# A planned transformer kernel: unread matmuls by share of the array, a finer table for VectorE's banks, a reserve behind a bank's last operation

## The chip, the core and the metric

The kernel runs on one core of a Trainium2 chip. The metric is the device time of one execution in microseconds; the table below gives three runs of the kernel before. TensorE (PE) multiplies matrices into PSUM, ScalarE (ACT) does the exponentials, VectorE (DVE) copies, adds and normalizes, GpSimd (POOL) takes a small share, and SyncE (SP) issues DMA transfers. Each engine works through its own queue in order.

## The reference

Two layers over a sequence of 2048 tokens of 448 numbers, each of an attention part with 16 heads of 28 and a dense part with a hidden width of 1792, both behind a layer norm and added to their input. The same weights serve both layers.

```python
def _A_ref(x, wqkv, wo):
    ...
    q, k, v = qkv[0], qkv[1], qkv[2]
    scores = jnp.einsum("bhqd,bhkd->bhqk", q, k) * Dh ** -0.5
    p = _softmax(scores, axis=-1)
    o = jnp.einsum("bhqk,bhkd->bhqd", p, v)
    return (lambda x, *d: x.transpose(*d))(o, 0, 2, 1, 3).reshape(B, S, D) @ wo

def _B_ref(x, w1, b1, w2, b2):
    h = jnp.einsum("bsd,df->bsf", x, w1) + b1
    r = jnp.where(h > zero, h, zero)
    h = r * r
    return jnp.einsum("bsf,fd->bsd", h, w2) + b2

x = A_x
x = x + _A_ref(_layernorm(x, axis=-1), A_wqkv, A_wo)
x = x + _B_ref(_layernorm(x, axis=-1), B_w1, B_b1, B_w2, B_b2)
x = x + _A_ref(_layernorm(x, axis=-1), A_wqkv, A_wo)
x = x + _B_ref(_layernorm(x, axis=-1), B_w1, B_b1, B_w2, B_b2)
```

## The kernel before

**Units, groups and banks.** The queries are cut into blocks of 256 (the last two of layer 1 of 128). A *unit* is 512 columns of scores: one head, one block of queries and two tiles of 128 keys (four tiles in the 128-query blocks). There are 2048 units in all, 1024 for each layer. A unit's scores fill one bank of PSUM. `s_stream` (L859) issues the score matmuls of a *group* of three units at a time (L924). A head has 28 numbers, padded to 32, so a score matmul uses 32 of the array's 128 rows, and those of different heads lie in different strips of rows. `e_stream` (L940) lets ScalarE compute the exponential of the group's banks in one instruction (L954). `p_stream` (L1044) multiplies the exponentials with the values, four heads side by side in strips of 32 columns (L1095), and one more column of ones gives the sums of the softmax.

**Banks that go to VectorE.** ScalarE need not take all three banks: `apart` (L815) decides, as a group is issued, whether a third unit is handed to VectorE. Then ScalarE's instruction has two banks. `a_unit` (L995) and `a_rest` (L1012) compute that bank's exponential with bit arithmetic: a shift and a maximum on VectorE (L1002), a product on GpSimd (L1019), a square (L1025) and a final sum on VectorE (L1032). Among the conditions of `apart` are a free set of scratch buffers, a busy share of VectorE of at most `BUSY` over 11 us, no bank among the last `STOP` units, and the table: `PACE[i * len(PACE) // len(units)]` (L840), in us, is the most that VectorE's backlog may hold when unit i is issued. With 64 entries, one holds for 32 units.

**The order of work.** The program is laid out by a planner (`Planner`, L140) while it is built. Every piece of work is an `Op` with an engine, a planned duration, what it depends on and which buffer it takes and releases. Streams of ops stand side by side with priorities (scores 0, exponentials 1, attention-value 2, then normalization, projections and dense parts, `sums` 9.1, `heat` 9.5); `run` (L193) takes again and again the op that can start first by the planner's own clocks. `earliest` (L163) computes when an op's inputs are there: the end of each, its `lat`, and a latency of its engine. Two ops with `port=True` on VectorE and GpSimd are not planned at the same time. The order so found is the order of each engine's queue; on the chip the engines then wait for each other by semaphores. So a changed planned duration changes no instruction, only the order.

**Dense work.** `layernorm` (L520), `qkv` (L681), `chain` (L1234) and `mm_tile` (L634, matmuls at L655) do the projections and the dense part of a block of tokens while the attention of other blocks goes on. VectorE copies their results out of PSUM: keys at L678, queries at L674, values at L706, relu at L1289, the square at L1296, the residual sum at L1231. `sums` (L375) adds up the columns of w1 for the tail, with matmuls against a single column of ones (L387), once the queries of layer 1 are there.

**Unread matmuls.** The planner adds matmuls that nobody reads. First, `s_stream` can issue the score matmuls of a group up to `MORE` = 3 more times into the same banks, where TensorE would be idle anyway and the exponentials of the group before still run (L911 to L916). Second, `heat` (L1501) issues one or two matmuls into a spare bank behind a group (L1516). Both look at `load` (L154), TensorE's planned busy share over the last microseconds: repetitions below 0.9 over 3.4 us (0.8 for the last 100 units), `heat` below 0.76 over 2.8 us.

**The tail.** After the last group of scores `finish` (L1329) and `ends_last` (L1436) carry the last block through its projection, norm and dense part.

Of the kernel before, what the change touches and what calls it, by code (L numbers as in the profile page):

```python
# [26 lines left out]
GY = 0.65  # L27
# [17 lines left out]
ENDU = 100  # L45
HOTE = 0.8
# [9 lines left out]
WINDOW = 2.8  # L56
# [19 lines left out]
PACE = (3.6, 2.2, 2.2, 1.8, 1.8, 1.8, 1.8, 3.0, 0.3, 0.9, 2.2, 2.2, 2.2, 1.4, 1.4, 1.4, 1.4, 1.4, 1.4, 2.2, 2.2, 2.2, 2.2, 1.4, 3.0, 3.0, 2.2, 2.2, 2.2, 1.8, 4.5, 4.5, 2.6, 2.6, 3.0, 3.0, 3.0, 3.6, 3.0, 1.4, 3.0, 4.5, 4.5, 4.5, 1.4, 1.4, 0.9, 1.4, 0.3, 1.4, 1.4, 1.4, 2.2, 2.2, 1.8, 1.8, 1.8, 1.8, 2.6, 2.6, 1.8, 1.8, 0.3, 6.0)  # L76
# [4 lines left out]
HOT = 0.9  # L81
MORE = 3
HEAT = 0.76
HWIN = 3.4
# [39 lines left out]
class Op:  # L124
    __slots__ = ("eng", "dur", "fn", "deps", "acq", "rel", "mode", "sets", "start", "end", "res", "turn", "ready", "lat", "need", "got", "more", "room", "port")

    def __init__(self, eng, dur, fn, deps=(), acq=None, rel=None, mode="full", sets=(), lat=0.0, need=1, port=False):
        self.eng = eng if isinstance(eng, tuple) else (eng,)
        self.dur, self.fn, self.deps, self.mode, self.lat = dur, fn, deps, mode, lat
        self.rel = rel if isinstance(rel, list) else ([] if rel is None else [rel])  # L130
        self.acq = acq if isinstance(acq, tuple) or callable(acq) else (() if acq is None else (acq,))
        self.sets = sets if isinstance(sets, list) else ([sets] if sets else [])
        self.start = self.end = self.res = self.turn = None
        self.need, self.got, self.more, self.port = need, [], 0.0, port
# [5 lines left out]
class Planner:  # L140
# [3 lines left out]
    def __init__(self):  # L144
        self.clock = {"PE": 0.0, "ACT": 0.0, "DVE": 0.0, "POOL": 0.0, "DMA": 0.0, "-": 0.0}
        self.mode = None
        self.tok = {}
        self.streams = []
        self.past = {"PE": [], "DVE": []}
        self.ports = {"POOL": [], "DVE": []}  # L150
        self.turns = lambda: False
        self.slack = lambda: SLACK
# [5 lines left out]

    def spawn(self, prio, gen):
        self.streams.append([prio, gen, next(gen, None)])  # L160
        self.streams.sort(key=lambda s: s[0](0.0) if callable(s[0]) else s[0])

    def earliest(self, o):  # L163
        t = 0.0
        for d in o.deps:
            if not isinstance(d, Op):
                d = self.tok.get(d)
            if d is None or d.end is None:
                return None, None
            same = d.eng[0] == o.eng[0] and len(o.eng) == 1  # L170
            t = max(t, d.end + d.lat + ((0.03 if same else 0.10) if d.eng[0] == "DVE" else
                                (0.0 if same and d.eng[0] != "DMA" else LAT[d.eng[0]])))
# [20 lines left out]
    def run(self):  # L193
        while self.streams:
# [46 lines left out]
def kernel(  # L241
# [278 lines left out]
    def layernorm(t0, nt, deps_of, early=False, mv=None, place=None, x_in=None, parts=False):  # L520
# [9 lines left out]
        for a, b in [(0, 1), (1, 2)] if single else [(0, nt)]:  # L530
# [9 lines left out]
            pl.spawn(EV, iter([rs]))  # L540
        box = {}
# [68 lines left out]
        for p0 in range(0, nt, wide):  # L610
# [4 lines left out]
            for j in js:  # L615
                xn = xns[2 * (own.turn % 2) + j % 2]

                def norm(e, j=j, xn=xn):
                    nc.vector.tensor_scalar(out=xn[:, 0:D], in0=x_sb[:, t0 + j, :],  # L619
                                            scalar1=mv[0][:, j, 0:1], scalar2=ln[j],  # L620
                                            op0=ALU.subtract, op1=ALU.mult)
                nm = Op("DVE", 0.39, norm, deps=[rss[j], *([] if x_in is None else [x_in])], sets=[("n", t0, j)] if early else (), port=True)
                yield nm
                xs.append((xn, nm))
# [234 lines left out]
    def s_stream():  # L859
        while at[0] < len(units):  # L860
# [5 lines left out]
            def fn(e, gi=gi, us=us, js=js):  # L866
# [44 lines left out]
                short = (HOT if len(units) - at[0] > ENDU else HOTE) - pl.load(HWIN)  # L911
# [4 lines left out]
                o.more = 0.22 * again  # L916
                for i in list(range(4)) * (again + 1):
# [94 lines left out]
    def a_rest(gi, c, box, unit):  # L1012
# [7 lines left out]
        y = Op("POOL", GY, part, deps=[c, ("p", gi)] if own else [c], acq=None if own else lambda: pd_free(unit), port=True)  # L1020
# [13 lines left out]
        o = Op("DVE", 0.683, close, deps=[h], rel=c, sets=("x", gi), port=True)  # L1034
# [9 lines left out]
    def p_stream():  # L1044


        for pi, (l, qb, g, kbs, first, last) in enumerate(passes):
# [19 lines left out]
            while todo:  # L1067
# [16 lines left out]
                def fn(e, now=now, begin=begin, close=close, box=box, pi=pi, l=l, g=g, r=r, n=n):  # L1084
# [4 lines left out]
                    for kb in now:  # L1089
# [15 lines left out]
                       rel=[gbuf[gi]["p" if w == "e" or gbuf[gi]["in"] else w] for w, gi in by], mode="col")  # L1105
                box.setdefault("o", o)
# [79 lines left out]
    def norm_pair(l, qb, g, pair):  # L1186
# [34 lines left out]
        def mul(e):  # L1221
            nc.vector.tensor_tensor(out=oTn_of[l, qb][0][:, g:g + 2, 0:n], in0=both,  # L1222
                                    in1=box["r"][:, :, 0:n], op=ALU.mult)
        m = Op("DVE", 0.13 + 2 * n / 930, mul, deps=[r, oTn_of[l, qb][1]], rel=pair["own"], port=True)
# [9 lines left out]
    def chain(l, qb):  # L1234
# [43 lines left out]
        for f0 in range(0, NFC, pack):  # L1278
# [11 lines left out]
            def square(e, b=b, w=w, f0=f0):  # L1290
                r = b["r"][:, 0:w].rearrange("p (f q) -> p f q", q=n)
                b["h"] = h = hidden(f0 // pack)
                if e == "ACT":
# [4 lines left out]
            def then(o, b=b, square=square):  # L1298
                aside = not s_left and (l, qb) == (1, len(blocks[1]) - 2)
                b["s"] = Op("ACT" if aside else "DVE", 0.5 if aside else 0.42, square, deps=[o], rel=o, port=True)  # L1300
# [200 lines left out]
    def heat():  # L1501


        for gi in itertools.count(HFROM):
# [63 lines left out]
```

## Time and profile before

| what | us |
|---|---|
| three runs: median (lowest, highest) | 845.75 (845.54, 848.41) |
| the profiled execution | 845.42 |
| its span, first to last instruction | 843.6 |
| ScalarE busy in the span | 821.3 |
| TensorE busy | 806.6 |
| VectorE busy | 783.8 |
| GpSimd busy | 225.3 |
| HBM traffic | 19 GB/s, mean over the span |

The mean clock granted to TensorE is 0.994 of the full one. The profile has views that the text uses: the busy shares of the engines; groups of instructions by line and shape (busy time, mean duration of one, idle time of the engine before them and what ended it); the span cut into stretches (busy time and count for each engine, granted clock, DMA); the waits in total; and the instructions in order of time. The names are those of the program: `sc` scores, `pt` exponentials, `oT` attention output, `mt` a dense result, `v_w` the scratch of a bank on VectorE. PEld is the loading of weights, which goes beside matmuls.

### The profile page before, as it was taken

What the parts mean: (1) busy time and instruction counts of PE and PEld (TensorE: products, weight loads), DVE (VectorE), ACT (ScalarE), POOL (GpSimd) and SP (SyncE); (2) the same over time, 40 slices, a digit from 0 to 9 for tenths busy, and PEclk for the clock granted to TensorE, in tenths of its full rate; (3) what the DMA queues carried; (4) which work ended last, traced back from release to release, by engine and by line L of the source; (5) the groups of instructions that cost most, each with busy time, mean ns of one, the idle gap of its engine ahead of it and who ended that gap; (6) DMA issues with size and microseconds to landing.
All of it is one profiled execution on the core that took longest, in us unless ns stands there. A gap on an engine that the chain in (4) does not pass through costs nothing.

```text
span 843.6 us, 28341 instructions
## 1 busy us (share of the span) xinstructions
PE 806.6 (96%) x12255; PEld 428.6 (51%) x12255; DVE 783.8 (93%) x1610; ACT 821.3 (97%) x700; POOL 225.3 (27%) x354
## 2 busy tenths in 40 slices
PE   8999999999999999999999999989999999999997
PEld 4455545554545455455445444534554545545565
DVE  7999989999989999999999999989989999999955
ACT  8998999999999999999999999989999999999994
POOL 3222322223222233222332333332222222232300
PEclk9999999999999999999999999989999999999999
DMA  9200000000000000000000000011000000000000
GB/s 251 68 3 2 25 20 15 16 15 15 15 3 16 15 15 16 7 11 15 2 2 3 2 2 3 11 30 32 18 23 21 20 26 15 14 25 16 17 11 18
DMA packets 32365, 17.98 MB, mean 21 GB/s; under 512 B 17833, under 2 KB 31787, under 8 KB 32240
## 3 DMA queue, kind: packets, MB, share of 16 engines
q1 hardware_dynamic: 32240, 16.18, 6.9%
q8 instruction: 95, 1.56, 0.8%
q14 instruction: 30, 0.25, 0.1%
HBM read 13.88 MB, written 2.07 MB: 19 GB/s over the span
## 4 chain that ended last, share of the span: by engine, by line
PE 44%; DVE 27%; ACT 22%; issue 5%; DMA 1%; POOL 0%; SPq 0%; ACTq 0%; DVEq 0%
ACT pt L954 22%; PE mt L655 18%; PE sc L924 15%; PE oT L1095 8%; DVE v_w L1002 3%; DVE pt L1032 2%; DVE r L1289 2%; DVE V_sb L1032 2%; DVE K_sb L1002 2%; DVE pt L1025 2%; DVE V_sb L1025 1%; PE mt L1516 1%; DVE xn L619 1%; DVE oTn L1222 1%; DVE Q_sb L674 1%
## 5 line engine op out<-in xcount | busy, mean ns | idle before, releaser
L954 ACT ACTIVATE pt<-sc 128x1536 bf16<-128x1536 f32 (+1 forms) x683 | 810.0, 1377 | 9.1 <-PE sc L924 8.0
L924 PE MATMUL sc<-Q_sb,K_sb 32*128 32x256 bf16 (+1 forms) x5258 | 308.6, 267 | 22.3 <-ACT pt L954 17.1
L924 PEld LDWEIGHTS <-K_sb 32*128 32x128 bf16 x5258 | 131.1, 92 | 202.5 <-issue 157.5
L1095 PE MATMUL oT<-pt,V_sb 128*32 128x256 bf16 (+1 forms) x4008 | 154.2, 270 | 1.2 <-DVE pt L1032 0.7
L1002 DVE TENSOR_SCALAR v_w<-sc 128x512 f32<-128x512 f32 x187 | 127.4, 683 | 10.7 <-PE sc L924 9.9
L655 PE MATMUL mt<-xnT,w 128*128 128x256 bf16 (+1 forms) x888 | 118.6, 271 | 0.9 <-DVE xnT L571 0.4
L1095 PEld LDWEIGHTS <-V_sb 128*32 128x32 bf16 x4352 | 91.4, 96 | 50.9 <-issue 47.7
L655 PEld LDWEIGHTS <-w 128*128 128x128 bf16 x896 | 74.9, 98 | 35.6 <-issue 27.3
L1019 POOL TENSOR_SCALAR V_sb<-v_w 128x512 bf16<-128x512 uint16 x74 | 54.2, 733 | 131.1 <-DVE v_w L1002 130.3
L1289 DVE TENSOR_SCALAR r<-mt 128x512 bf16<-128x512 f32 x108 | 73.9, 684 | 6.3 <-PE mt L655 5.9
L1019 POOL TENSOR_SCALAR pt<-v_w 128x512 bf16<-128x512 uint16 x69 | 46.2, 670 | 114.0 <-DVE v_w L1002 91.4
L655 PE MATMUL mt<-w,V_sb 128*128 128x448 bf16 (+1 forms) x288 | 70.5, 349 | 0.0
L1002 DVE TENSOR_SCALAR K_sb<-sc 128x512 f32<-128x512 f32 x73 | 49.8, 683 | 4.6 <-PE sc L924 4.5
L1032 DVE SCALAR_TENSOR_TENSOR V_sb<-v_w,V_sb 128x512 int16<-128x512 f32 x74 | 51.5, 698 | 0.1
L1032 DVE SCALAR_TENSOR_TENSOR pt<-v_w,pt 128x512 int16<-128x512 f32 x69 | 47.7, 694 | 0.1
L1231 DVE TENSOR_TENSOR x_sb<-x_sb,mt 128x448 bf16<-128x448 bf16 x62 | 37.9, 612 | 8.7 <-PE mt L655 8.4
L1025 DVE TENSOR_TENSOR pt<-pt 128x512 bf16<-128x512 bf16 x99 | 45.1, 468 | 0.7 <-POOL pt L1019 0.7
L1025 DVE TENSOR_TENSOR V_sb<-V_sb 128x512 bf16<-128x512 bf16 x89 | 41.4, 474 | 2.5 <-POOL V_sb L1019 2.5
L1019 POOL TENSOR_SCALAR pt<-K_sb 128x512 bf16<-128x512 uint16 x30 | 21.6, 719 | 71.9 <-DVE K_sb L1002 51.5
L509 DVE BATCH_NORM_STATS2 st<-x_sb 128x6 f32<-128x448 bf16 x63 | 38.7, 616 | 1.2 <-DMA x_sb<-in_A_x_dram 0.7
L1516 PE MATMUL mt<-xn,ident 128*128 128x448 bf16 x105 | 36.5, 364 | 0.9 <-DVE oT_sb L1123 0.3
L655 PEld LDWEIGHTS <-V_sb 128*128 128x128 bf16 x302 | 24.3, 98 | 25.2 <-issue 12.1
(143 smaller groups left out, 882.1 us busy)
## 6 DMA issues: line engine op xcount, KB each, us to landing
rec<-scr SPq DMA_DIRECT2D x54, 128.0 KB
x_sb<-in_A_x_dram SPq DMA_DIRECT2D x8, 224.0 KB
out_dram<-x_sb SPq DMA_DIRECT2D x15, 112.0 KB
w<-in_B_w_dram SPq DMA_DIRECT2D x1, 1568.0 KB
w<-in_B_w_dram SPq DMA_DIRECT2D x1, 1344.0 KB
dn<-oT_sb SPq DMA_DIRECT2D x54, 4.0 KB
V_sb<-in_A_wqkv_dram SPq DMA_DIRECT2D x4, 168.0 KB
scr<-dn SPq DMA_DIRECT2D x27, 8.0 KB
```

Source lines behind the costliest of these rows:

```text
L509: nc.vector.bn_stats(out=box["st"][:, :], in_=x_sb[:, t0 + j, :] if src is None else src())
L655: nc.tensor.matmul(box["t"][:, c0:c0 + n], lhsT=lhsT() if callable(lhsT) else lhsT, rhs=rhs, start=a, stop=b)
L924: nc.tensor.matmul(dst[k][:, i * nt * P:(i + 1) * nt * P], lhsT=K_sb[l][rows, g, (kb + i) * P:(kb + i + 1) * P], rhs=Q_sb[rows, g, t0 * P: ...
L954: t = nc.scalar.activation(out=pt[:, 0:n], in_=gbuf[gi]["sc"][:, 0:n], func=AF.Exp, scale=float(np.log(2.0)) * 2.0 ** -FRAC)
L1002: t = nc.vector.tensor_scalar(out=box["w"], in0=two(src), scalar1=EXP_SHIFT, scalar2=EXP_LOW, op0=ALU.add, op1=ALU.max)
L1019: nc.gpsimd.tensor_scalar(out=two(pd), in0=low, scalar1=-EXP_MID * 65536, scalar2=EXP_BEND, op0=ALU.add, op1=ALU.mult)
L1025: nc.vector.tensor_tensor(out=pd, in0=pd, in1=pd, op=ALU.mult)
L1032: nc.vector.scalar_tensor_tensor(out=two(pd.bitcast(DT.int16)), in0=box["w"], scalar=EXP_BITS, in1=two(pd), op0=ALU.add, op1=ALU.add)
L1095: nc.tensor.matmul(box["t"][DHP * hh:DHP * hh + DHP, 0:n], lhsT=V_sb[l][:, kb + i, 4 * g + hh, :], rhs=p[:, c0:c0 + n], start=begin and kb ...
L1231: nc.vector.tensor_tensor(out=x_sb[:, tb, lo:hi], in0=x_sb[:, tb, lo:hi], in1=t[:, 0:hi - lo], op=ALU.add)
L1289: nc.vector.tensor_scalar(out=r[:, 0:w], in0=t[:, 0:w], scalar1=0.0, scalar2=None, op0=ALU.max)
L1516: nc.tensor.matmul(t[:, 0:D], lhsT=ident[:, :], rhs=xns[0][:, 0:D], start=True, stop=True)
```

## The change

Three things change in the planner's decisions.

- Unread matmuls: `load` is replaced by `warm`, the share of the array used over the last `TICK` = 1.8 us of the plan. Each op on TensorE adds a weight `w`: 0.0533 us for each unit of scores and each pass, 0.2133 for each step of attention-value, and 0.9 (`SHARE`) of the planned duration for every other op. Both kinds of unread matmuls are added below 0.55 (`WARM`, `WARM2`).
- The table `PACE` has 128 entries in place of 64, with other values; one now holds for 16 units.
- Planned times in `a_rest`: the product on GpSimd takes 0.617 in place of 0.65 with 0.05 behind it (`YL`), and the last sum on VectorE has 0.25 behind it (`XL`), which counts for what reads it and for the buffers that it releases.

`earliest` keeps the time of an op's inputs once it is known. Options to put the norm, the pair product and some squares on GpSimd come in and are off (`NORMG`, `GM_ON`, `GS_ON` = 0).

```diff
-GY = 0.65
+GY = 0.617
+XL = 0.25
+TICK = 1.8
+WARM = 0.55
+WARM2 = 0.55
+SHARE = 0.9
+YL = 0.05
...
-PACE = (3.6, 2.2, 2.2, 1.8, 1.8, 1.8, 1.8, 3.0, 0.3, 0.9, 2.2, 2.2, 2.2, 1.4, 1.4, 1.4, 1.4, 1.4, 1.4, 2.2, 2.2, 2.2, 2.2, 1.4, 3.0, 3.0, 2.2, 2.2, 2.2, 1.8, 4.5, 4.5, 2.6, 2.6, 3.0, 3.0, 3.0, 3.6, 3.0, 1.4, 3.0, 4.5, 4.5, 4.5, 1.4, 1.4, 0.9, 1.4, 0.3, 1.4, 1.4, 1.4, 2.2, 2.2, 1.8, 1.8, 1.8, 1.8, 2.6, 2.6, 1.8, 1.8, 0.3, 6.0)
+PACE = (2.2, 2.2, 2.2, 2.2, 1.8, 2.2, 2.2, 1.4, 3.0, 1.4, 1.4, 1.4, 2.2, 3.2, 3.6, 2.2, 2.2, 2.2, 2.2, 2.2, 0.6, 3.4, 2.6, 1.8, 1.0, 1.8, 2.6, 2.6, 2.2, 3.8, 3.0, 2.2, 2.2, 3.6, 2.2, 0.6, 3.0, 1.8, 1.8, 1.8, 1.8, 2.6, 2.2, 2.2, 1.4, 3.4, 2.6, 1.0, 2.2, 3.4, 3.6, 3.6, 1.4, 2.2, 3.0, 2.6, 3.8, 3.4, 1.8, 1.0, 2.6, 2.6, 2.2, 2.2, 3.8, 3.0, 1.8, 1.0, 3.8, 3.0, 1.8, 2.2, 2.2, 1.4, 3.2, 4.4, 2.6, 3.6, 3.6, 1.4, 1.8, 3.6, 3.0, 3.0, 3.0, 3.0, 2.2, 2.2, 2.2, 2.2, 3.0, 3.0, 1.8, 2.2, 2.6, 2.6, 1.4, 1.4, 4.0, 3.6, 3.6, 1.8, 1.8, 2.2, 2.2, 3.6, 1.4, 1.4, 2.2, 4.0, 1.8, 1.4, 2.2, 1.8, 2.6, 2.6, 2.2, 2.2, 2.6, 2.2, 2.8, 3.2, 1.4, 1.8, 1.8, 2.2, 2.2, 2.2)
...
+    def warm(self):
+
+        now = self.clock["PE"]
+        return sum(w * (min(e, now) - max(s, now - TICK)) / (e - s) for s, e, w in self.used if e > now - TICK and s < now) / TICK
...
+            if e == "PE" and o.end > s:
+                self.used = [u for u in self.used if u[1] > s - 2 * TICK] + [(s, o.end, SHARE * o.dur if o.w is None else o.w)]
...
-                short = (HOT if len(units) - at[0] > ENDU else HOTE) - pl.load(HWIN)
+                short = WARM2 - pl.warm()
...
+                o.w = 0.0533 * len(us) * (again + 1)
...
-        y = Op("POOL", GY, part, deps=[c, ("p", gi)] if own else [c], acq=None if own else lambda: pd_free(unit), port=True)
+        y = Op("POOL", GY, part, deps=[c, ("p", gi)] if own else [c], acq=None if own else lambda: pd_free(unit), port=True, lat=YL)
...
-        o = Op("DVE", 0.683, close, deps=[h], rel=c, sets=("x", gi), port=True)
+        o = Op("DVE", 0.683, close, deps=[h], rel=c, sets=("x", gi), port=True, lat=XL)
...
+                o.w = 0.2133 * len(now)
...
-            short = HEAT - pl.load(WINDOW)
+            short = WARM - pl.warm()
...
-            k = 1 if short < 0.14 else 2
+            k = 1 if short < 0.055 else 2
```

More of the change, by code (lines that the diff above doesn't have):

```diff
@@ L149, in __init__ @@
         self.past = {"PE": [], "DVE": []}
+        self.used = []
         self.ports = {"POOL": [], "DVE": []}
@@ L163, in earliest @@
     def earliest(self, o):
[L164 to L172, printed above, removed]
+        t = o.base
+        if t is None:
+            t = 0.0
+            for d in o.deps:
+                if not isinstance(d, Op):
+                    d = self.tok.get(d)
+                if d is None or d.end is None:
+                    return None, None
+                same = d.eng[0] == o.eng[0] and len(o.eng) == 1
+                t = max(t, d.end + d.lat + ((0.03 if same else 0.10) if d.eng[0] == "DVE" else
+                                    (0.0 if same and d.eng[0] != "DMA" else LAT[d.eng[0]])))
+            o.base = t
         acq = o.acq() if callable(o.acq) else o.acq
@@ L540, in layernorm, with turned @@
             pl.spawn(EV, iter([rs]))
+            if not parts and NORMG and not early:
+                def turned(e, a=a, b=b):
+                    ln["m"] = mv[0][:, 2:4, 0]
+                    nc.vector.tensor_scalar(out=ln["m"][:, a:b], in0=mv[0][:, a:b, 0], scalar1=-1.0, scalar2=None, op0=ALU.mult)
+                ng = Op("DVE", 0.165, turned, deps=[mv[1][b - 1]])
+                yield ng
         box = {}
```

37 lines of the change are left out of this document (24 added, 13 removed).

## The prediction

> **What bounds the kernel now.** I read the busy shares and the waits first, then the groups by form, then the span cut into stretches. All durations are those of the profiled execution, 845.42 us, of which the span is 843.6 and 1.8 lies around it; the median of the runs is 845.75, so a gain found in the span is taken off 845.75 unchanged.
>
> ```profile
> PE 806.6 (96%) x12255; PEld 428.6 (51%) x12255; DVE 783.8 (93%) x1610; ACT 821.3 (97%) x700; POOL 225.3 (27%) x354
> ...
> L954 ACT ACTIVATE pt<-sc 128x1536 bf16<-128x1536 f32 (+1 forms) x683 | 810.0, 1377 | 9.1 <-PE sc L924 8.0
> ```
> ```profile
> L954 ACT ACTIVATE pt<-sc 128x1536 bf16<-128x1536 f32 x422 | 607.8, 1541 | 4.7 <-PE sc L924 4.0 <-PE oT L1095 0.3
> L924 PE MATMUL sc<-Q_sb,K_sb 32*128 32x256 bf16 x4746 | 291.5, 273 | 20.0 <-ACT pt L954 15.0 <-DVE K_sb L1002 1.1 <-DVE oTn L1222 0.5
> L954 ACT ACTIVATE pt<-sc 128x1024 bf16<-128x1024 f32 x261 | 278.7, 1113 | 4.4 <-PE sc L924 4.0 <-ACT pt L954 0.3
> ...
> L1516 PE MATMUL mt<-xn,ident 128*128 128x448 bf16 x105 | 36.5, 364 | 0.9 <-DVE oT_sb L1123 0.3 <-DVE V_sb L706 0.2 <-DVE more L1121 0.2
> ```
>
> ScalarE sets the time. It runs 683 groups of exponentials, 422 over three banks and 261 over two; the third bank of each of those 261 went to VectorE. A group always takes three units, so the count of groups is fixed (2048 units), and the only thing that shortens ScalarE's own work is the number of two-bank groups: each one more is worth 1541 - 1113 = 428 ns.
>
> ```profile
> 10.70:63.90 53.20, 51.88 (x736) 27.31 (x733) 51.04 (x117) 53.09 (x43) 12.49 (x25) 1.00 0.30 86
> 63.90:117.30 53.40, 50.91 (x759) 28.21 (x760) 51.95 (x102) 50.15 (x44) 14.75 (x20) 1.00 0.05 13
> 117.30:168.50 51.20, 48.76 (x752) 26.44 (x748) 46.31 (x95) 50.74 (x44) 12.08 (x20) 1.00 0.07 18
> 168.50:220.20 51.70, 50.57 (x760) 26.99 (x752) 49.51 (x100) 51.45 (x44) 13.24 (x22) 1.00 0.05 13
> 220.20:271.30 51.10, 49.71 (x753) 26.46 (x747) 45.90 (x92) 51.10 (x44) 13.73 (x22) 1.00 0.05 13
> 271.30:320.80 49.50, 47.76 (x707) 24.83 (x703) 48.13 (x98) 49.50 (x43) 14.32 (x25) 1.00 0.05 13
> ...
> 371.90:423.30 51.40, 48.76 (x748) 25.79 (x741) 50.26 (x105) 50.37 (x44) 15.81 (x22) 1.00 0.03 7
> 423.30:472.50 49.20, 47.40 (x711) 24.22 (x710) 47.82 (x95) 48.88 (x43) 14.53 (x23) 1.00 0.01 2
> ...
> 523.00:573.80 50.80, 47.11 (x690) 22.41 (x690) 47.13 (x97) 48.61 (x44) 18.97 (x27) 0.90 0.08 19
> 573.80:624.70 50.90, 48.52 (x741) 24.54 (x742) 48.17 (x99) 50.88 (x44) 11.21 (x17) 1.00 0.10 27
> 624.70:675.80 51.10, 49.66 (x732) 27.01 (x724) 47.00 (x93) 51.10 (x44) 11.96 (x18) 1.00 0.07 19
> ...
> 726.40:775.50 49.10, 47.83 (x708) 25.07 (x701) 47.89 (x98) 49.10 (x43) 12.35 (x19) 1.00 0.06 18
> ...
> 829.20:843.60 14.40, 10.72 (x133) 7.82 (x130) 7.56 (x26) 3.08 (x7) 0.56 (x1) 1.00 0.06 18
> ```
>
> These stretches are sixteenths of the units (some 43 groups each); after the length come the busy times of PE, PEld, DVE, ACT and POOL, then the clock. From 10.7 to 829.2 us the exponentials take 810.0 (both forms with their overlaps removed, the page's row of L954); so only about 818.5 - 810.0 = 8.5 us of ScalarE are idle there, and they sit in few places: 3.25 in the stretch from 63.9, 1.03 in that from 371.9, 2.19 in that from 523.0. The 10.7 us ahead and the 14.4 behind are the start and the tail. TensorE's 96% is no bound: part of it is matmuls that nobody reads.
>
> ```profile
> ACT pt L954 <- PE sc L924: 8.0, 12, 3.1
> ```
> ```profile
> 67.48 9.76 ACT L954 ACTIVATE pt<-sc 128x1536 bf16<-128x1536 f32 x8
> 80.34 1.94 ACT L954 ACTIVATE pt<-sc 128x1024 bf16<-128x1024 f32 x2 [3.10 <-PE sc L924]
> ```
> ```profile
> 79.19 0.69 DVE L678 CAST K_sb<-mt 128x512 bf16<-128x512 f32 x1 [0.19 <-PE mt L655]
> ```
>
> All waits of ScalarE's exponentials for scores come to 8.0 us in 12 places, and one of them is 3.10: the scores issued at 79.84 need keys that VectorE copies at 79.19 to 79.88.
>
> **Change, part 1: unread matmuls.** Their number is in the rows above. The 256-column score matmuls needed are 2 for each of 1920 units (the other 128 units lie in blocks of one row tile and use the 128-column form), 3840; 4746 were issued, so 906 are repetitions, about 151 passes of six. To them come 105 of L1516. A repeated pass costs
>
> ```profile
> 69.18 0.40 PE L924 MATMUL sc<-Q_sb,K_sb 32*128 32x256 bf16 x6 [0.25 <-ACT pt L954]
> ...
> 70.24 0.83 PE L924 MATMUL sc<-Q_sb,K_sb 32*128 32x256 bf16 x18
> ```
>
> (0.83 - 0.40) / 2 = 0.22 us, so 33 us, and the 105 about 36.5 us of busy time, of which some goes beside other work. The new rule asks not how long PE was busy but how much of the array's rows and columns it used over 1.8 us, and adds below 0.55. Counted so (a score or attention-value matmul a quarter, a projection 0.9), the three-unit groups alone make 0.16 of 1.2 us, attention-value as much: 0.27; projections carry the rest. My count over the whole trace with the repetitions left out is a mean near 0.6, and under 0.55 in about a fifth of the trailing 1.8 us looks (an estimate from the columns and rows of the matmul rows). Some 150 passes lay behind about a fifth of the groups before. So I expect the unread work to fall moderately, from about 70 us to between 30 and 60, moved into the stretches without projections. What it frees on PE is worth 0: scores are early except at the 12 waits, and repetitions are only put where the planner sees PE idle and ScalarE still has a bank to read. If that cover is gone, one pass too many costs its 0.22 us, once.
>
> The price of a clock drop is visible, since there is one:
>
> ```profile
> 540.60:544.00 3.40, 3.40 (x53) 2.30 (x52) 3.19 (x8) 3.40 (x4) 1.43 (x2) 1.00 0.02 5
> 544.00:545.70 1.70, 1.70 (x40) 1.37 (x43) 1.70 (x5) 1.70 (x3) 0.00 (x0) 1.00 0.09 5
> 545.70:552.50 6.80, 6.29 (x80) 2.26 (x72) 4.78 (x12) 5.66 (x5) 1.34 (x2) 0.50 0.15 42
> 552.50:555.90 3.40, 2.10 (x41) 1.10 (x40) 3.40 (x8) 3.40 (x5) 2.01 (x3) 1.00 0.04 2
> 555.90:559.30 3.40, 3.40 (x40) 0.98 (x34) 3.40 (x8) 3.16 (x3) 1.44 (x2) 0.50 0.19 64
> 559.30:562.70 3.40, 3.03 (x49) 1.54 (x50) 2.51 (x6) 2.65 (x4) 1.28 (x2) 0.99 0.10 21
> ```
> ```profile
> 120.00:124.00 4.00, 3.12 (x55) 1.79 (x50) 2.58 (x7) 4.00 (x4) 0.00 (x0) 1.00 0.13 34
> ```
> ```profile
> 542.40 1.13 PE L387 MATMUL mt<-onec,w 128*128 128x1 bf16 x16
> 543.47 0.39 PE L924 MATMUL sc<-Q_sb,K_sb 32*128 32x256 bf16 x6
> 543.80 1.13 PE L387 MATMUL mt<-onec,w 128*128 128x1 bf16 x16
> ```
>
> The clock halves at 545.7 after PE had been busy without a gap, and stays full at 120 us with PE busy 3.12 of 4. What was different are the one-column matmuls of `sums` (L387, 16 in 1.13 us): they occupy PE and stream next to nothing. ScalarE's idle time from 545.7 to 562.7 is 1.14 + 0 + 0.24 + 0.75 = 2.13 us, so three cold windows of 3.4 us cost about 0.7 us each. Does the change mend it? It gives attention-value and score operations a share of their own, but `sums` keeps the default, 0.9 of its planned duration, so the new count sees the same full array there as the old one. I take 0 for it, with 2.1 us of gain and 2.1 of loss (three more cold windows elsewhere) as the bounds.
>
> [...]
>
> **Part 2: the table.** PACE bounds the backlog of VectorE, in us, above which no further bank is given to it. It goes from 64 entries (mean 2.23) to 128 (mean 2.38). By sixteenths the old means are low in the third, fourth, fifth, twelfth and thirteenth, 1.4, 1.6, 1.6, 1.27, 1.12; the new ones are 2.15, 2.40, 2.12, 2.45, 2.48. In the same stretches VectorE idles 4.89, 2.19, 5.20, 2.73 and 4.10 us by the rows, 19.1 together, while the ones with higher entries idle 1.14 (371.9), 1.38 (423.3), 1.37 (271.3), 1.21 (726.4). A bank costs VectorE
>
> ```profile
> L1002 DVE TENSOR_SCALAR v_w<-sc 128x512 f32<-128x512 f32 x187 | 127.4, 683 | 10.7 <-PE sc L924 9.9
> ...
> L1032 DVE SCALAR_TENSOR_TENSOR pt<-v_w,pt 128x512 int16<-128x512 f32 x69 | 47.7, 694 | 0.1
> ...
> L1025 DVE TENSOR_TENSOR pt<-pt 128x512 bf16<-128x512 bf16 x99 | 45.1, 468 | 0.7 <-POOL pt L1019 0.7
> ```
>
> 0.683 + 0.468 + 0.694 = 1.85 us. Filling the five to 1.3 idle each gives 19.1 - 6.5 = 12.6 us, 6.8 banks. Against it the eighth and eleventh go down (3.25 to 2.45, 4.12 to 2.73), perhaps 2 banks. Elsewhere the old table was no lower than the new. Bounds: minus 5 (a smoother table, same DVE work, banks late) and plus 13 (every stretch at 1.3 us idle, without the start and the last). I take 6 banks: 6 x 0.428 = 2.6 us.
>
> The second effect of a finer table is where banks are not given. The 3.10 us wait at 77 to 80 lies in a stretch with VectorE at 51.95 of 53.4, its banks and the key copies in one queue; a bank fewer ahead of it moves the keys up by 1.85 us. New entries there swing between 1.4 and 3.6 where all old ones were 1.8 or 3.0. Of the 4.1 us of idle time in the stretches from 63.9 and 371.9 I take 60% as gone, 2.5 us; bounds 0 and 4.1, and a loss of 3.1 for each such wait made anew.
>
> **Part 3: the reserve.** The plan's Pool part goes from 0.65 to 0.617 plus 0.05 behind it, 0.017 later in all; the last operation of a bank (L1034) counts 0.25 us later for whoever reads it and for its buffer. Instructions are the same; only their order moves. Now TensorE waits for that operation
>
> ```profile
> L1095 PE MATMUL oT<-pt,V_sb 128*32 128x256 bf16 (+1 forms) x4008 | 154.2, 270 | 1.2 <-DVE pt L1032 0.7
> ```
>
> 0.7 us in all with pt as output, off ScalarE's path. I take 0; bounds plus 0.7 (those waits were on the path) and minus 0.7 (as much again, buffers 0.25 later, a few banks refused). The options that come with 0 (norms, squares and pair products on GpSimd) and the kept base time in `earliest` change no instruction: 0.
>
> **Sum.** 2.6 + 2.5 + 0 + 0 = 5.1 us; 845.75 - 5.1 = 840.6, put at 840.5.
>
> **Rivals.** (a) Everything falls well: 13 banks (5.6), both waits (4.1) and the drop at 545 (2.1) gone, 11.8 us: 834. For it: VectorE idles that much; against it: `sums` is counted as before. (b) The banks gained are given back: VectorE's copies for keys, values and relu come later by the deeper backlog, so 2.6 is lost to waits for scores of about 0.3 us, and the stalls only move: 845. For it: the order is planned anew everywhere, and VectorE is at 93% already. (c) Slower, by VectorE's queue: with an allowance near 2.4 us in stretches that had 1.1 to 1.6, a bank stands ahead of copies that feed the next scores. A wait like that at 77 us costs 3.1; from one more such wait on the banks' gain is gone, and three more make 845.75 - 2.6 + 9.3 = 852.5. For it: the 3.10 us wait exists where VectorE is fullest; against it: the fuller stretches from 271.3 and 726.4 have ScalarE idle 0.0 (49.50 of 49.50, 49.10 of 49.10). (d) Slower, by the clock: the old rule topped up wherever PE was not 0.9 busy, the new one stops at 0.55 by plan, where transposes and one-column matmuls count as 0.9. From nine cold windows on (6.3 us) the gain is gone; twenty make 845.75 - 5.1 + 14 = 855. Against it: at 0.78 busy (120 us) the clock held.
>
> **How the numbers follow.** A measurement tells about 0.5% (4.2 us) from no change: below 841.5 is faster, over 850 slower. Forecast 0.42 (its own range 837 to 843.5, six sevenths of it below 841.5), (a) 0.12, (b) 0.24, (c) 0.14, (d) 0.08. Faster 0.36 + 0.12 = 0.48; same 0.06 + 0.24 = 0.30; slower 0.14 + 0.08 = 0.22. The range reaches from (a) to near the time of (c), 834 to 852, and leaves out (d) and some half of (c), 0.15.
>
> **What would show it.** Two-bank groups near 267 instead of 261, and DVE above 47.5 us in the stretches from about 117, 220, 574 and 625; ScalarE's wait for scores below 6 us with none of 3 us; the clock at 1.00 but for one drop while L387 runs; L924 with fewer than 5258 matmuls; a tail of about 14.4 us. The forecast is wrong if the two-bank groups stay at 261 or fewer, if waits on keys or on `xnT` grow, or if cold windows appear away from L387.

## The result, and the profile after

| | before | after |
|---|---|---|
| median of 4 runs (lowest, highest), us | 846.06 (845.54, 848.41) | 836.04 (834.38, 836.43) |
| ratio, with its 95% interval | 1 | 0.9873 (0.9849 to 0.9896) |
| span of the profiled execution | 843.6 | 834.4 |

The kernel became faster by 1.3%, some 10 us. The page of the kernel after, busy times first (the lines have moved: L954 is now L986, L924 is L956, L1516 is L1552, L387 is L406, L655 is L686):

```profile
PE 780.0 (93%) x11403; PEld 405.6 (49%) x11403; DVE 793.5 (95%) x1646; ACT 815.2 (98%) x700; POOL 234.8 (28%) x366
...
L986 ACT ACTIVATE pt<-sc 128x1536 bf16<-128x1536 f32 (+1 forms) x683 | 803.8, 1407 | 4.3 <-PE sc L956 3.3
L956 PE MATMUL sc<-Q_sb,K_sb 32*128 32x256 bf16 (+1 forms) x4412 | 278.4, 267 | 36.0 <-ACT pt L986 28.6
```

The groups by form:

```profile
L986 ACT ACTIVATE pt<-sc 128x1536 bf16<-128x1536 f32 x410 | 592.5, 1577 | 2.8 <-PE sc L956 2.2 <-PE oT L1127 0.2
L986 ACT ACTIVATE pt<-sc 128x1024 bf16<-128x1024 f32 x273 | 291.7, 1152 | 1.5 <-PE sc L956 1.2
...
L1552 PE MATMUL mt<-xn,ident 128*128 128x448 bf16 x99 | 29.5, 367 | 0.0
```

And sixteenths of the units, with the same columns as in the prediction (PE, PEld, DVE, ACT, POOL, clock):

```profile
63.90:114.50 50.60, 46.43 (x687) 25.37 (x684) 49.88 (x98) 50.37 (x45) 12.77 (x18) 1.00 0.06 15
114.50:164.40 49.90, 47.53 (x673) 25.09 (x662) 47.53 (x101) 49.90 (x43) 14.80 (x21) 1.00 0.06 17
164.40:214.80 50.40, 48.76 (x683) 25.03 (x681) 50.23 (x103) 50.40 (x45) 15.52 (x24) 1.00 0.05 13
214.80:265.80 51.00, 47.75 (x687) 24.26 (x686) 50.07 (x101) 50.54 (x44) 15.03 (x25) 1.00 0.05 13
...
514.70:566.00 51.30, 46.56 (x673) 21.83 (x675) 49.01 (x99) 49.28 (x44) 17.84 (x24) 0.87 0.08 21
566.00:615.60 49.60, 46.34 (x656) 23.44 (x650) 48.78 (x101) 49.60 (x44) 13.19 (x20) 1.00 0.10 27
615.60:665.80 50.20, 48.08 (x672) 24.50 (x670) 49.85 (x100) 50.20 (x44) 13.41 (x20) 1.00 0.06 17
...
818.30:834.40 16.10, 11.92 (x144) 8.59 (x142) 7.89 (x27) 3.21 (x7) 0.56 (x1) 1.00 0.05 15
```

The span lost 9.2 us, and the rows account for it. Exponentials: 810.0 to 803.8, minus 6.2, of which 12 more two-bank groups (261 to 273) at 428 ns are 5.1. ScalarE's idle time between its first and last exponential: 8.5 to 3.6 (from 10.9 to 818.3 us, 807.4 less 803.8), minus 4.9. The tail: 14.4 to 16.1, plus 1.7. The start: plus 0.2. VectorE's idle time in the five stretches with low old entries fell from 19.1 us to 4.6 (2.37, 0.17, 0.93, 0.82 and 0.35). The score matmuls fell to 4412, so just 60 are repetitions (4412 - 512 - 3840), where 906 were before; those of `heat` stayed, 99 to 105. The clock is halved over one stretch (0.50 from 529.3 to 542.9 us), and `sums` (L406, from 525.3 us) leads into it. The waits of ScalarE for scores are 3.3 us, none over 0.7.

### The profile page after: what moved, and what is told of

It is laid out like the page before. It is cut to its first block, busy times and chain, and to the rows that moved or that the text cites. A ratio compares the mean times of both kernels' runs of the same rounds, so it can differ in the third digit from the quotient of the medians.

```text
span 834.4 us, 26688 instructions
## 1 busy us (share of the span) xinstructions
PE 780.0 (93%) x11403; PEld 405.6 (49%) x11403; DVE 793.5 (95%) x1646; ACT 815.2 (98%) x700; POOL 234.8 (28%) x366
## 4 chain that ended last, share of the span: by engine, by line
DVE 40%; ACT 26%; PE 25%; issue 8%; DMA 0%; POOL 0%; ACTq 0%; DVEq 0%
ACT pt L986 26%; PE mt L686 10%; PE sc L956 8%; DVE v_w L1034 6%; DVE pt L1064 5%; PE oT L1127 4%; DVE r L1322 4%; DVE pt L1057 3%; DVE K_sb L1034 3%; DVE V_sb L1064 2%; DVE x_sb L1264 2%; DVE V_sb L1331 1%; DVE h L1064 1%; DVE V_sb L1057 1%; DVE xn L649 1%
## 5 line engine op out<-in xcount | busy, mean ns | idle before, releaser
L986 ACT ACTIVATE pt<-sc 128x1536 bf16<-128x1536 f32 (+1 forms) x683 | 803.8, 1407 | 4.3 <-PE sc L956 3.3
L956 PE MATMUL sc<-Q_sb,K_sb 32*128 32x256 bf16 (+1 forms) x4412 | 278.4, 267 | 36.0 <-ACT pt L986 28.6
L956 PEld LDWEIGHTS <-K_sb 32*128 32x128 bf16 x4412 | 106.6, 92 | 213.3 <-issue 154.7
L1034 DVE TENSOR_SCALAR v_w<-sc 128x512 f32<-128x512 f32 x194 | 131.2, 681 | 4.1 <-PE sc L956 3.3
L686 PE MATMUL mt<-xnT,w 128*128 128x256 bf16 (+1 forms) x872 | 116.4, 272 | 3.6 <-DVE r L1322 0.9
L1051 POOL TENSOR_SCALAR pt<-v_w 128x512 bf16<-128x512 uint16 x85 | 61.4, 723 | 158.6 <-DVE v_w L1034 138.5
L686 PEld LDWEIGHTS <-w 128*128 128x128 bf16 x896 | 75.8, 98 | 37.2 <-issue 28.2
L1051 POOL TENSOR_SCALAR V_sb<-v_w 128x512 bf16<-128x512 uint16 x54 | 39.2, 726 | 101.6 <-DVE v_w L1034 101.4
L686 PE MATMUL mt<-w,V_sb 128*128 128x448 bf16 x260 | 66.9, 355 | 0.0
L1064 DVE SCALAR_TENSOR_TENSOR pt<-v_w,pt 128x512 int16<-128x512 f32 x85 | 57.2, 680 | 0.0
L1034 DVE TENSOR_SCALAR K_sb<-sc 128x512 f32<-128x512 f32 x78 | 52.9, 680 | 2.4 <-PE sc L956 1.9
L1057 DVE TENSOR_TENSOR pt<-pt 128x512 bf16<-128x512 bf16 x109 | 49.1, 463 | 0.0
L1057 DVE TENSOR_TENSOR V_sb<-V_sb 128x512 bf16<-128x512 bf16 x89 | 40.1, 460 | 0.0
L1051 POOL TENSOR_SCALAR V_sb<-K_sb 128x512 bf16<-128x512 uint16 x35 | 24.6, 703 | 51.7 <-DVE K_sb L1034 44.3
L1064 DVE SCALAR_TENSOR_TENSOR V_sb<-v_w,V_sb 128x512 int16<-128x512 f32 x54 | 37.5, 694 | 0.1
L686 PEld LDWEIGHTS <-V_sb 128*128 128x128 bf16 x302 | 24.5, 98 | 25.7 <-issue 12.6
L1051 POOL TENSOR_SCALAR h<-v_w 128x512 bf16<-128x512 uint16 x29 | 20.5, 708 | 45.1 <-DVE v_w L1034 44.3
```

The lines of the kernel that those rows point to most:

```text
L686: nc.tensor.matmul(box["t"][:, c0:c0 + n], lhsT=lhsT() if callable(lhsT) else lhsT, rhs=rhs, start=a, stop=b)
L956: nc.tensor.matmul(dst[k][:, i * nt * P:(i + 1) * nt * P], lhsT=K_sb[l][rows, g, (kb + i) * P:(kb + i + 1) * P], rhs=Q_sb[rows, g, t0 * P: ...
L986: t = nc.scalar.activation(out=pt[:, 0:n], in_=gbuf[gi]["sc"][:, 0:n], func=AF.Exp, scale=float(np.log(2.0)) * 2.0 ** -FRAC)
L1034: t = nc.vector.tensor_scalar(out=box["w"], in0=two(src), scalar1=EXP_SHIFT, scalar2=EXP_LOW, op0=ALU.add, op1=ALU.max)
L1051: nc.gpsimd.tensor_scalar(out=two(pd), in0=low, scalar1=-EXP_MID * 65536, scalar2=EXP_BEND, op0=ALU.add, op1=ALU.mult)
L1057: nc.vector.tensor_tensor(out=pd, in0=pd, in1=pd, op=ALU.mult)
```

## The experiments

Each ran beside the kernel before; the ratios are to it. "Planned anew" means that an edit changes one planned duration or one choice, whereupon the planner lays out all that follows in another order.

**One part undone, and a change of no part.** Three edits of the kernel after take one part back each; the fourth, `a_null`, touches none and shifts one planned duration by a thousandth of a microsecond.

```diff
a_null     -GY = 0.617
           +GY = 0.616
a_rule     -short = WARM2 - pl.warm()
           +short = (0.9 if len(units) - at[0] > 100 else 0.8) - pl.load(3.4)
           -short = WARM - pl.warm()
           +short = 0.76 - pl.load(2.8)
           -k = 1 if short < 0.055 else 2
           +k = 1 if short < 0.14 else 2
a_table    PACE: the 64 entries of before
a_reserve  -GY = 0.617, XL = 0.25, YL = 0.05
           +GY = 0.65, XL = 0.0, YL = 0.0
```

> The changed kernel with GY 0.616 in place of 0.617: no part of the change undone, but the planner lays the work out anew from the first tie that falls otherwise. Theory 'parts': the gain comes from the parts, so nothing is lost, 836 plus or minus 1.5 us, and some 273 two-bank groups. Theory 'fit': the table is fitted to one exact plan, so any other plan loses part of the gain, 839 to 844 us, with fewer than 273 two-bank groups and new waits of ScalarE for scores.

> The changed kernel with the old rule for unread matmuls (busy share, 0.9 and 0.76). Theory 'parts' of the prediction: what the rule frees on TensorE is worth nothing, so 836 to 838 us with about 900 repeated score matmuls back. Theory 'fit': as much lost as by the null, 839 to 844. A third theory, that repeated matmuls cost time by delaying real ones: 846 or more, and ScalarE's waits for scores back at 8 us.

> The changed kernel with the old table of 64 entries. Theory 'parts': the table carries both terms of the predicted gain, so nearly all of it is lost, 843 to 846 us, some 262 two-bank groups. Theory 'fit': no more than by the null, 839 to 844.

> The changed kernel with the old planned times of a bank (GY 0.65, nothing behind it, nothing behind the last operation). Theory 'parts': 0, so 836 to 837 us. Theory 'fit': as the null, 839 to 844.

| | median, us | ratio (95%) |
|---|---|---|
| a_null | 845.69 | 0.9986 (0.9970 to 1.0002) |
| a_rule | 857.29 | 1.0129 (1.0114 to 1.0144) |
| a_table | 847.83 | 1.0015 (0.9997 to 1.0032) |
| a_reserve | 851.22 | 1.0039 (1.0021 to 1.0058) |

The prediction's theory, that each part brings a gain of its own to the time, falls here: a kernel with all three parts and a plan that differs by a thousandth is no faster than the kernel before. Nor does a_reserve fit either theory: it lies above the range of both. Forms and tail of a_null:

```profile
L986 ACT ACTIVATE pt<-sc 128x1024 bf16<-128x1024 f32 x268 | 284.4, 1146 | 3.5 <-PE sc L956 3.4
```
```profile
10.50:826.60 816.10, 762.95 (x11201) 392.72 (x11198) 777.21 (x1572) 807.70 (x683) 227.87 (x346) 0.99 0.07 19
826.60:844.60 18.00, 13.10 (x178) 10.29 (x175) 8.15 (x27) 5.27 (x11) 0.56 (x1) 1.00 0.05 15
```

Its first 296 us of VectorE's work are those of the kernel after in the same order; then a bank's shift (L1034) and a square (L1057) stand the other way round, and from there the rest differs. It has 5 two-bank groups fewer (exponentials 807.7, plus 3.9), 8.4 us of idle time in place of 3.6 (816.1 less 807.7, plus 4.8) and a tail of 18.0 (plus 1.9), less 0.4 at the start: the 10.2 us between the spans of 844.6 and 834.4. The loss builds up from there. About 5 us of it come between the 450th and the 500th exponential, in a_null from about 545 to 609 us: ScalarE idles 3.9 us there, and 0.1 in the kernel after. a_null has a second stretch of half clock there, 10.2 us long from 561.7, and 1.7 us of that idle time lie in it. The three undone parts can't be read against 836, then, but only against other plans that nobody picked. So measured, a_table and a_reserve lie 2 and 6 us from a_null, and a_rule 12 us.

**The kernel before, planned anew; and the rule alone.** `b_null` asks whether the kernel before was a picked plan too, `b_rule` puts the new rule alone into it (table and reserve of before, so planned anew as well).

```diff
b_null  -GY = 0.65
        +GY = 0.651
b_rule  -short = (HOT if len(units) - at[0] > ENDU else HOTE) - pl.load(HWIN)
        +short = 0.55 - pl.warm()
        -short = HEAT - pl.load(WINDOW)
        +short = 0.55 - pl.warm()
        -k = 1 if short < 0.14 else 2
        +k = 1 if short < 0.055 else 2
        +o.w = ..., pl.warm, pl.used as in the change
```

> The kernel before with GY 0.651 in place of 0.65: nothing of the change, only a new layout from the first tie that falls otherwise. Theory 'fit' (which the changed kernel's own such run has raised): the old table is fitted to its exact plan as well, so this loses some 8 us or more against the kernel before. The planner's own last clock, printed while a program is built, was 5 to 11 us under the measured time for the six plans so far; it is 853 here against 838 for the kernel before, which would make 858 to 863 us. Theory 'only the new table is brittle': 846 plus or minus 2 us.

> The kernel before with the new rule for unread matmuls alone; table and planned times of before. Theory 'planned room': in the plan a repetition occupies TensorE, and a projection that comes up meanwhile no longer fits ahead of the next scores, so under the old rule the dense work falls behind the attention and the border of the layers (near 526 us) stands open, unless the plan was picked to avoid it. Then this untuned plan with the new rule lies far below the untuned one with the old rule (862.8): 844 to 849 us, no wait of 10 us, and some 1300 dense matmuls issued by the 400th exponential against 1240. Theory 'the rule does nothing to the time': 855 to 863.

b_null took 862.78 us (1.0176, 1.0142 to 1.0210), b_rule 846.37 (1.0000, 0.9984 to 1.0015). Both came as the theories of fit and of planned room had them: against this one shifted plan the kernel before owed 1.8%, some 15 us, to its exact plan, and the rule alone makes an untuned plan as fast as that one. The planner's last clock (the end of its latest op, printed as the program is built) kept to what the expectation says of it: in the eleven plans that were run it lay 4 to 11 us under the median (b_null 853.2, f_old 852.9 and 864.05, s_best 829.3 and 833.44).

**No table picked at all.** `f_new` and `f_old` have a single entry of 2.2; only the rule differs between them.

```diff
f_new  PACE = (2.2,)
f_old  PACE = (2.2,), and the three lines of a_rule
```

> The changed kernel with one entry of 2.2 for the whole table: no table picked at all, new rule, new reserve. Theory 'planned room': 843 to 849 us, no long wait at the border, the loss against 836 being that the plan wasn't picked. Theory 'the finer table is worth several us whatever the plan': the same, so this run alone doesn't tell; it tells with the next one.

> The same single entry of 2.2 and the new reserve, with the old rule for unread matmuls. Neither plan was picked, so the difference to the run beside it is the rule's. Theory 'planned room': 856 to 863 us, some 13 us above it, with a wait of ScalarE near 526 us of 8 to 11 us, and fewer than 1270 dense matmuls issued by the 400th exponential. Theory 'the rule does nothing': within 3 us of it.

f_new took 842.97 us (0.9959, 0.9947 to 0.9971) and f_old 864.05 (1.0210, 1.0184 to 1.0236), 21 us apart where some 13 were expected. ScalarE's instructions around the border of the layers, f_old:

```profile
519.28 7.31 ACT L986 ACTIVATE pt<-sc 128x1536 bf16<-128x1536 f32 x6 [0.45 <-PE sc L956]
538.57 7.86 ACT L986 ACTIVATE pt<-sc 128x1024 bf16<-128x1024 f32 x7 [11.98 <-PE sc L956]
```

the same stretch of f_new:

```profile
516.36 16.64 ACT L986 ACTIVATE pt<-sc 128x1536 bf16<-128x1536 f32 x14 [0.18 <-PE sc L956]
533.23 1.02 ACT L986 ACTIVATE pt<-sc 128x1024 bf16<-128x1024 f32 x1 [0.23 <-PE sc L956]
```

and the same in b_null and in a_rule, whose rule is the old one:

```profile
536.87 8.47 ACT L954 ACTIVATE pt<-sc 128x1024 bf16<-128x1024 f32 x8 [10.36 <-PE sc L924]
```
```profile
536.14 1.94 ACT L986 ACTIVATE pt<-sc 128x1024 bf16<-128x1024 f32 x2 [10.49 <-PE sc L956]
```

What ScalarE waits for in f_old stands in VectorE's queue, in order of time: the residual sum of layer 0's last block, its moments, its norm, the transposed copy, the keys of layer 1, and then scores again.

```profile
530.23 0.62 DVE L1264 TENSOR_TENSOR x_sb<-x_sb,mt 128x448 bf16<-128x448 bf16 x1 [0.49 <-PE mt L686]
530.88 0.63 DVE L528 BATCH_NORM_STATS2 st<-x_sb 128x6 f32<-128x448 bf16 x1
...
532.81 0.70 DVE L649 TENSOR_SCALAR xn<-x_sb,mv,rstd 128x448 bf16<-128x448 bf16 x2 [1.08 <-POOL rstd L556]
534.00 0.69 DVE L596 COPY xnT<-tp 128x1024 bf16<-128x1024 bf16 x1 [0.49 <-PE tp L584]
536.47 0.69 DVE L709 CAST K_sb<-mt 128x512 bf16<-128x512 f32 x1 [1.77 <-PE mt L686]
```

The attention of layer 0 is over at 526 us, and layer 1 can't begin, since its keys hang on a chain that ends at 537. That chain is late because the dense work before it is. The dense matmuls (L686 alone) from 10 to 490 us, f_old first, then f_new:

```profile
10.00:490.00 480.00, 209.93 (x1218) 98.57 (x1216) 1.00 0.07 20
```
```profile
10.00:490.00 480.00, 217.08 (x1300) 107.61 (x1298) 1.00 0.07 20
```

82 matmuls fewer have been issued. Counted by progress of the attention it is the same: by the 400th exponential f_old has issued 1238, b_null 1240 and a_rule 1258, and f_new 1317, a_null 1322, a_table 1322, a_reserve 1297, b_rule 1296 and the kernel after 1309. The kernel before, with the old rule and its picked plan, has 1291 and no wait at the border. So the old rule pushes the dense work back, and the plan of before hid it. The mechanism that fits is in the code: a repetition adds 0.22 us to TensorE's clock in the plan (`o.more`), and a projection is placed only if it ends by the time the next scores are due, so what came up meanwhile goes behind one more group. The lag is shown; that it comes in by just this line was not tried by itself, nor was the share of `heat`, of which the three kernels with the old rule and a new plan have 135 to 140 matmuls and the five with the new rule 105 to 122.

So of the 19.7 us between the spans (860.7 and 841.0) 12.0 are this wait; the rest is in smaller waits for scores (22.8 us of them in all, 7.4 in f_new) and in the tail (19.0 against 15.3 us from the last exponential's end to the end of the span).

Eight of these plans were picked by nobody, and together they say more than any pair, since a new plan alone moves the time by several us. The three with the old rule (a_rule, b_null, f_old) have ratios of 1.0129 to 1.0210 and leave ScalarE idle for 19.3 to 24.9 us between its first and last exponential. The five with the new rule (a_null, a_table, a_reserve, b_rule, f_new) have 0.9959 to 1.0039 and 6.9 to 14.4 us. The number of two-bank groups follows the table instead: 259 to 263 in the four plans with the old table (before, b_null, b_rule, a_table), 268 to 273 in the four with the new one (after, a_null, a_rule, a_reserve), 266 and 271 with the single entry.

**Repetitions left out of a plan that stays.** `b_norep` keeps the plan of before and doesn't issue the 906 repetitions; `a_noemit` keeps the plan of after and issues neither its 60 repetitions nor its 99 matmuls of `heat`.

```diff
b_norep   -for i in list(range(4)) * (again + 1):
          +for i in range(4):
a_noemit  the same, and
          -for _ in range(k):
          +for _ in range(0):
```

> The kernel before with its plan untouched, but the 906 repeated score matmuls not issued (their planned time stays as a hole). Theory 'repeats are free': the same time, 845 to 847 us, the clock full but near 546. Theory 'repeats delay real matmuls': 840 to 844, with fewer waits of ScalarE for scores. Theory 'repeats hold the clock': the share of the array falls in some 15 thin stretches, more cold windows, each about 0.7 us of ScalarE, 848 to 856 us.

> The changed kernel with its plan untouched, but none of its unread matmuls issued, neither the 60 repetitions nor the 99 of heat. If the few that the new rule leaves are needed for the clock: several more cold windows than the one stretch at 529, 840 us or more. If even these are not needed: 835 to 837 us and no cold window elsewhere.

b_norep took 845.38 us (0.9987, 0.9967 to 1.0007): on a given order the 906 repetitions cost nothing and give nothing. In the profiled executions it got colder, 24 us of half clock in place of 10, but the executions of one kernel differ in this: the mean granted clock was 0.982 to 0.990 in those of b_norep, and 0.987 to 0.994 in those of the kernel before beside it. a_noemit took 846.71 (0.9984, 0.9954 to 1.0014), 1.1% or some 10 us more than with its unread matmuls. Its profiled execution, the longest of ten (851.30), was at half clock for 65 us in place of 14, in seven stretches; the ten have mean clocks of 0.961 to 0.976, where the kernel after has 0.992 to 0.995. That much of the time hangs on the few that the new rule keeps. The two longest stretches of a_noemit:

```profile
538.00:565.30 27.30, 23.48 (x288) 9.11 (x277) 25.39 (x53) 24.69 (x23) 10.65 (x12) 0.50 0.11 28
572.10:585.70 13.60, 13.08 (x117) 5.69 (x117) 7.89 (x15) 9.57 (x8) 1.46 (x3) 0.50 0.07 21
```

Where the clock fell in b_norep (its windows, then those of the kernel before at the same place):

```profile
117.00:120.40 3.40, 2.27 (x52) 1.13 (x51) 3.40 (x9) 3.40 (x3) 1.74 (x3) 1.00 0.15 44
120.40:127.20 6.80, 5.78 (x44) 2.59 (x43) 3.90 (x9) 6.20 (x6) 0.00 (x0) 0.56 0.10 21
```
```profile
117.00:120.40 3.40, 3.07 (x75) 1.82 (x69) 3.29 (x9) 3.40 (x4) 1.30 (x2) 1.00 0.16 55
120.40:127.20 6.80, 5.76 (x81) 3.43 (x80) 4.50 (x10) 6.35 (x6) 0.62 (x1) 1.00 0.09 17
```

**The one-column sums.** `a_hot` keeps the plan of after and puts one unread 448-column matmul behind each pair of sums but the last; `s_best` counts the sums as no use of the array (`last.w = 0.0`) and has another table, found by trying entries and keeping those that make the planner's last clock smaller.

```diff
a_hot   +if fcs[0] < NFC - 2:
        +    nc.tensor.matmul(box["t"][:, 32:480], lhsT=ident[:, :], rhs=xns[0][:, 0:D], start=False, stop=False)
s_best  +last.w = 0.0
        PACE: 128 other entries
```

> The changed kernel with its plan untouched and one unread 448-column matmul more behind each pair of one-column sums (13 in all, some 0.19 us each). Theory 'array share': the 13.7 us of half clock behind 529 us go or shrink to 7 at most, and ScalarE's idle time of 1.9 us from 529 to 543 with them, 834 to 836 us. Theory 'busy time' (the clock follows how long TensorE is busy): the drop stays, and 2.5 us more of work in a full stretch makes 836 to 839.

> The changed kernel with the one-column sums counted as no use of the array, and a table picked for the resulting plan by its own last clock, which is 2 us under that of the changed kernel. Theory 'picked plan': the chip follows the plan, 832 to 836 us, and the half clock near 530 us is shorter than 13.7 us. If the plan's last clock says nothing so close to its least: anything from 834 to 845.

a_hot took 835.23 us (0.9865, 0.9837 to 0.9893), the same as the kernel after within the intervals. It added six matmuls and not the thirteen of its expectation: the sums go in seven pairs, and the trace has six. Its profiled execution still had a cold stretch, from 531.8 in place of 529.3 and 10.2 us long in place of 13.7, with TensorE busy 3.40 of the 3.40 us from 528.6. But two of its four executions had a mean granted clock of 1.000, no cold stretch at all, and took 834.42 us each; the other two, with 0.995 and 0.994, took 836.04 and 837.41. So the expectation (the stretch goes or shrinks to 7 us) was met in two of the four, and the same order of work meets the drop in one execution and not in another. Within this kernel the stretch cost 1.6 to 3.0 us.

s_best took 833.44 us (0.9851, 0.9827 to 0.9876): the least of all, but its interval overlaps that of the kernel after, so the two can't be told apart. Its profiled execution, the longest of four, had 17.1 us of half clock from 524, against what was expected, at a mean clock of 0.990. The other three had 0.994 to 0.996, some 7 to 10 us (an estimate: twice the missing share of the span, which gives the 17 us for 0.990), and so kept to the expectation.

## Why the prediction was right, and where not

The direction and the range held (840.5 forecast, 834 to 852; 836.04 measured, of 846.06). That is in good part luck: by the prediction's mechanism a_null would have kept the gain, and it took 845.69. By its steps:

- **ScalarE sets the time, and a two-bank group is worth 428 ns.** Right: 12 groups and 4.9 us of idle time make up the gain.
- **The table, 6 banks, 2.6 us.** It measured 12 banks, 5.1 us. The stretches named (third, fourth, fifth, twelfth, thirteenth) were the ones that filled, down to 0.9 us of VectorE's idle time on average where 1.3 was assumed, and the loss of banks in the eighth and eleventh was outweighed. Two steps of the working were loose: 6.8 banks less 2 are 4.8 and not 6, and the old means are lower elsewhere too, by 0.05 to 0.25 in six more sixteenths. The banks are the table's doing: every plan with the new table has 268 or more, every plan with the old one 263 or fewer. That the time follows is not borne out: a_null has 7 more than the kernel before and gives it back in idle time and tail, and a single entry of 2.2 has 842.97.
- **Waits of ScalarE, 2.5 us.** In the two stretches that the term is for, the idle time fell from 4.3 us (3.25 and 1.03, where the prediction adds up 4.1) to 0.2, so it measured its upper bound; over the whole span the fall is 4.9. The 3.10 us wait at 77 us went altogether. In other plans it is at most 0.5 us with the new table and the new reserve (a_null, a_rule), 0.98 with the old table (a_table), 3.78 with the old reserve (a_reserve), and 3.6 to 3.9 in b_null, b_rule, f_new and f_old. So it goes with these two parts, in one or two plans each.
- **"What it frees on PE is worth 0."** This step failed. The prediction looked at the chip, where the repetitions really cost nothing (b_norep, 0.9987), and held that they are only put where the planner sees TensorE idle. It left out that the plan books their time, and that later work then finds no room: 12 us (a_rule against a_null), 15 (b_null against b_rule, by the ratios) and 21 (f_old against f_new) between plans that nobody picked. It also left out that the kernel before stood on its exact plan, worth some 15 us (b_null), which covered that loss; so the change replaced one well-fitting plan with another on better ground, and the net is 10. That both plans were found by picking is a reading of what one shifted plan for each loses (a_null, b_null).
- **The unread work falls to 30 to 60 us.** It came to some 32 us, inside the range at its lower end: 2.2 of repetitions (10 passes at 0.22) and 29.5 of `heat`. The split was not foreseen: `heat` stayed nearly whole, and the repetitions went from 906 to 60. Why so few are left, by the threshold or by the room in the plan, no run shows.
- **`sums` keeps its blind spot, 0.** Right: the one cold stretch leads off with L406, 13.7 us long after 10.2, and ScalarE idles 1.86 us in it (0.89 and 0.97, in the windows of the last section) after 2.13. That is 0.5 us for each cold window of 3.4 us, where the prediction read 0.7 off the kernel before.
- **The reserve, 0.** Not settled. a_reserve lies 5.5 us above a_null, but b_rule, without the reserve, is no slower than a_table, with it (1.0000 against 1.0015, the same table); a new plan changes as much by itself. The wait of 3.78 us above is the one piece of a_reserve that has a place.
- **A tail of 14.4.** It was 16.1; the plans that were run have 14.4 to 19.1.
- **Rivals.** (a), that all falls well, came nearest: 834 against 836, except that the drop stayed and the tail grew. (b), banks gained and given back, is what a_null looks like: 268 two-bank groups, waits for scores at 8.0 us as before, 845.69. (c) and (d), the slower ones, did not come: no new wait over 0.7 us, and no cold window away from `sums`. The mechanism of (d) shows in a_noemit, which had 65 us of half clock and took some 10 us more than the kernel after; the long waits that cost as (c) would are at the border in f_old, by late dense work and not by banks ahead of copies.

The two that remain open: how much of the picked plan's 7 to 10 us (836.04 against 842.97 and 845.69) could be had again for other shapes, and the reserve's own worth.

## What to carry to other kernels

Where a planner lays out the order, measure a change that should do nothing before crediting one that did something: here a thousandth of a microsecond in one planned duration cost 10 us in one kernel and 15 in the other. Compare rules between several plans that nobody picked (one entry for a whole table is a cheap way), and pick the plan last. Look at the granted clock of every execution, not at the profiled one alone. Work that is free on the engine (906 repetitions in b_norep, 0.9987) isn't free in a plan: filler that is booked as busy time pushes real work behind it, and here the bill came at the border between the layers.

## What the runs showed of the hardware

In the two profiled executions below, of the kernels before and after, the clock fell behind windows that used little of the array, in two of three cases with TensorE busy for 0.96 of the window or more. Windows of the kernel after around its drop (PE, PEld, DVE, ACT, POOL, clock), and two rows that time a column:

```profile
525.00:529.30 4.30, 4.17 (x80) 2.86 (x80) 4.30 (x10) 4.30 (x5) 0.34 (x1) 1.00 0.01 1
529.30:536.10 6.80, 6.80 (x98) 3.54 (x95) 6.09 (x13) 5.91 (x7) 2.35 (x4) 0.50 0.04 4
536.10:542.90 6.80, 6.80 (x72) 1.90 (x68) 5.44 (x13) 5.83 (x5) 2.33 (x4) 0.50 0.14 41
```
```profile
822.12 1.86 PE L686 MATMUL sc<-w,V_sb 128*128 128x448 bf16 x9
...
823.87 0.92 PE L686 MATMUL sc<-w,V_sb 128*128 128x448 bf16 x4
```

Nine matmuls less four are 0.94 us, so a column takes 0.94 / 5 / 448 = 0.42 ns. The shares that follow are an estimate from the matmul rows of these two profiles: each matmul counted as its columns times 0.42 ns times the share of the 128 x 128 places that it uses (a score matmul, 32*128, or an attention-value matmul, 128*32, a quarter), and the span from the first full clock (6.4 us in the kernel before, 7.0 in the kernel after) to 824 us cut into windows of 3.41 us that begin where the clock changes (the cold stretches last 6.8 and 3.4 us in the kernel before and 13.7 us in the kernel after, two, one and four such windows). Of the 469 windows at full clock the clock fell behind three:

| window, us | share of the array | TensorE's busy share |
|---|---|---|
| before, 542.3 to 545.7 | 0.24 | 1.00 |
| before, 552.5 to 555.9 | 0.31 | 0.62 |
| after, 525.9 to 529.3 | 0.33 | 0.96 |

Of those behind which it held, the least share was 0.41 before (538.9 to 542.3) and 0.43 after (542.9 to 546.3); where a matmul at a window's edge is put moves these shares by up to 0.03. Streamed columns alone, without the share of the places, don't part them: by that count the three have 0.94, 1.22 and 1.33 (matmuls in different strips overlap: four of 0.27 us start between 527.16 and 527.17 in the kernel after), and 3 and 56 windows that held in the kernel before, and 98 in the kernel after, have less. Nor does TensorE's busy share: it was 1.00 and 0.96 in two of the three, and 0.68 in a window where the clock held (before, 388.7 to 392.1, 2.32 of 3.40). Of the seven cold windows, those behind which the clock came back have shares of 0.37 and 0.41 (before) and 0.40 (after), those behind which it stayed low 0.28 (before), 0.22, 0.29 and 0.35 (after). One order of work does not meet the drop in every execution: the four of a_hot have mean granted clocks of 0.994, 0.995, 1.000 and 1.000.

The kernel's own threshold of 0.55 over 1.8 us lies above the shares of those three and of the seven cold ones; where the clock fell all the same, at `sums`, the plan had counted one-column matmuls at 0.9.
